# Scaled fp16 pairs in place of fp32r pairs in the projections of a gated two-branch attention kernel

## The chip, the cores and the metric

The kernel runs on one core of a Trainium2 chip. The time is device microseconds of one execution, on that core. A core has five engines that run their own instruction streams in order and meet at semaphores: TensorE (PE in the profile; its weight loads are listed apart as PEld), VectorE (DVE), ScalarE (ACT), GpSimdE (POOL) and SyncE (SP), which here only issues transfers. Matmuls write PSUM, which has eight banks of 512 fp32 columns; DVE and ACT read the results from there.

## The reference

Two attention branches read the same x (2048 tokens, 512 features) and are mixed by a gate. Both have 32 heads of 16 features.

```python
g = sigmoid((x * gate_w).sum(-1, keepdims=True))
a = A(x, wq, wk, wv, wo, beta)        # memory-augmented, four segments of 512 tokens
b = B(x, wqkv, wo_b)                  # plain softmax attention over all 2048 tokens
out = g * a + (1 - g) * b
```

In A, each segment has causal softmax attention inside the segment and a linear memory over the segments before it. With `phi(t) = t + 1 for t > 0, exp(t) otherwise`:

```python
q, k, v = x @ wq, x @ wk, x @ wv                 # split into heads and segments
a_dot = softmax(q @ k.T * 0.25 + causal) @ v
a_mem = (phi(q) @ M) / (phi(q) @ z + 1e-6)
o = sigmoid(beta) * a_mem + (1 - sigmoid(beta)) * a_dot
M, z = M + phi(k).T @ v, z + phi(k).sum()        # for the next segment
```

The weights of A's Q and K are larger than B's by a factor of 200, so the scores need about fp32 precision. All products with x are therefore made from pairs: each operand is split into a high and a low part, and three of the four products are summed (high-high, high-low, low-high).

## The kernel before, in words

x comes transposed, in four chunks of 512 tokens (`load_xt`), each as four slices of 128 features. The kernel has two stages.

The first stage, to about 375 us, makes the projections. `split_x` and `split` make the pairs: ACT copies the fp32 source into an fp32r tile (the high part), DVE subtracts that from the source (the low part). `v_job` projects 128 tokens onto all 512 columns of V with 12 matmuls (four feature slices times three products, `v_mm`, line 285) and ACT evicts the bank (line 293). `qk_job` projects one chunk of 512 tokens onto a group of 128 columns (8 heads) of Q or K with 12 matmuls (`qk_mm`, line 311). `qk_out` then turns the bank into an fp16 pair: ACT writes `st[:, 0] = b * sc` (line 323), DVE writes `st[:, 1] = b * sc - st[:, 0]` (line 326), where `sc` is a power of two per weight group, taken from the group's largest magnitude and x's. In A the same bank also gives phi: DVE takes the minimum with 0 (line 322), ACT the exponential of that, in place (line 325), and DVE adds the positive part (line 328). The pairs go to DRAM as images of Q and K, from which the attention reads.

The power of two comes from `x_abs` and `w_abs` (DVE: largest magnitude per partition), `w_top` (a matmul with the identity turns the column into a row, DVE takes the maximum) and `w_rng` (a matmul with ones spreads it over the partitions, DVE keeps the exponent bits and inverts). Only the outputs are scaled; the fp32r operands of the matmuls are not.

The order is written out by hand. First come the four slices of chunk 0 and of A's V weights: each is split as it lands, and its four matmuls, one for each of the first four V tiles, follow. Then come V tiles 0 to 15 of A; between them stand the splits of the next chunk, the gate's dot product (`dot_x`, DVE), the statistics, and POOL's weight loads. Then follow the eight Q and K jobs of B's first group, and 16 blocks (`blk`): each has one Q job and one K job of A, a read-out of the memory (`mem_out`, matmuls at line 397, which need phi of that block's Q job), its update (`mem_tr`, `mem_upd`, `mem_put`), and two or three jobs of B from the list `fill`. From block 4 on, `spill` strews score tasks of the first attention units among them (pairs of matmuls at line 535 with a DVE maximum at line 537). `misc` hands out PSUM banks, the least recently used first: eight in the V tiles, six in the first blocks, four from block 4 on.

The second stage is attention: for 32 steps, score matmuls (line 598), exponentials on ACT (line 604), products with V (line 620), and the maxima for the next step (lines 535 and 537). Nothing of it is touched by the change, but four last B jobs of `fill` stand in its first step.

Of the kernel before, what the change touches and what calls it, by code (L numbers as in the profile page):

```python
# [18 lines left out]
H = 32  # L19
# [10 lines left out]
TOP = 4.0  # L30
# [8 lines left out]
def gated_mix_kernel(ctx, tc, xt, wq, wk, wv, wo, beta, wqkv, wob, gate_w, out):  # L39
# [27 lines left out]
    XH = [xh[c // 2][:, c % 2] for c in range(NC4)]  # L67
# [3 lines left out]
    RAWV = [KBF[0][:, k] for k in range(4)] + flat + [RAW[:, n] for n in range(8)]  # L71
# [4 lines left out]
    XL = [X.tile([128, 4, C], FR, name=f"xl{c}") for c in range(NC4)]  # L76
    WV = [X.tile([128, 4, DM], FR, name=f"wv{s}") for s in range(2)]
    WS = [[[X.tile([128, 4, 128], FR, name=f"ws{w}{s}") for s in range(2)] for w in range(2)]]
# [7 lines left out]
    rng = P.tile([128, 2, 4, 2], FT, name="rng")  # L86
    xbd = P.tile([128, 1], FT, name="xbd")
# [35 lines left out]
    def raw_buf():  # L123
        i = cnt.get("raw", 0)
        cnt["raw"] = i + 1
        return RAWV[i if i < 6 else 6 + (i - 6) % 8]

# [13 lines left out]
    def constants():  # L141
# [10 lines left out]
        nc.vector.memset(ones, 1.0)  # L152
# [33 lines left out]
    def split_x(c, ks, eng=None):  # L186
        src = XS[c][:, ks]
        nc.scalar.activation(XH[c][:, ks], src, AF.Copy)
        nc.vector.tensor_tensor(XL[c][:, ks], src, XH[c][:, ks], op=OP.subtract)

# [67 lines left out]
    def load_wv(kd, k, eng=None):  # L258
        src, c0 = wcols(kd, 2)
        WR[k] = raw_buf()  # L260
        (eng or nc.gpsimd).dma_start(WR[k], src[k * 128:(k + 1) * 128, c0:c0 + DM])

    def split_wv(k):
        split(WV[0][:, k, :], WV[1][:, k, :], WR.pop(k))

# [9 lines left out]
    def split_w(n, kd, g, ws=(0, 1)):  # L275
        for w in ws:
            split(WS[n][w][0], WS[n][w][1], WR[kd, g][w])

# [9 lines left out]
    def v_out(b, kd, tt):  # L288
# [4 lines left out]
        nc.scalar.activation(vs[:, tl % 2, :, :E], b.rearrange("p (h e) -> p h e", h=H), AF.Copy)  # L293
# [21 lines left out]
    def qk_out(b, kd, g, w, c):  # L315

        sc = rng[:, "AB".index(kd), g, w:w + 1]
        st = X.tile([128, 2, C], HF, name="st", bufs=4)
        phi = kd == "A" and (c > 0 if w == 0 else c < NC4 - 1)
        if phi:  # L320
            ph = PHI[g, w, c] = X.tile([128, C], FT, name=f"phi{w}")
            nc.vector.tensor_scalar(ph, b, 0.0, None, op0=OP.min)
        nc.scalar.activation(st[:, 0], b, AF.Copy, scale=sc)  # L323
        if phi:
            nc.scalar.activation(ph, ph, AF.Exp)
        nc.vector.scalar_tensor_tensor(st[:, 1], b, sc, st[:, 0], op0=OP.mult, op1=OP.subtract)  # L326
        if phi:
            nc.vector.scalar_tensor_tensor(ph, b, 0.0, ph, op0=OP.max, op1=OP.add)
# [12 lines left out]

    def x_abs(c):
        if "x" not in ST:
            ST["x"] = X.tile([128, NC4], FT, name="xabs")
# [796 lines left out]
```

## Time and profile before

| | us |
|---|---|
| three runs | 1846.36, 1846.48, 1847.8 |
| median | 1846.48 |
| profiled execution | 1849.68 |
| its span, first to last instruction | 1848.0 |
| V tiles of A end, first B projection starts | 60.15 |
| PE busy | 1807.7 |
| DVE busy | 1591.2 |
| ACT busy | 1432.4 |
| POOL busy | 339.3 |

A row of the timeline gives the start, the time, the engine, the line of the kernel, the operation, what it writes and reads, and, in brackets, how long the engine stood idle before and what ended that wait. Several like instructions in a row are merged (x8); their time is from the first start to the last end. A matmul's row includes its way through the array, so the distance between starts is what a stream of them costs, not the row's time. A group of instructions has its total busy time and the mean of one in ns. The row of a tile or line has the shortest, median and longest time of one in ns. A row of the waits has the total, the number and the longest.

### The profile page before, as it was taken

How to read it: one execution, taken by the hardware profiler on the slowest of the kernel's cores; microseconds unless marked ns; L12 is line 12 of the kernel's file. 1: busy time of each engine (PE TensorE's matmuls, PEld its weight loads, DVE VectorE, ACT ScalarE, POOL GpSimd, SP SyncE). 2: the span in 40 equal slices, each digit the busy share in tenths (PEclk: the TensorE clock that was granted, in tenths of full speed). 3: DMA queues.
4: the chain of work that ended last, by engine and by line, in shares of the span. 5: the costliest groups of instructions: out<-in, count | busy, mean ns of one | idle time of the engine just before them, and what ended most of it. 6: DMA issues, size and time to landing. Idle time of an engine off the chain costs nothing.

```text
span 1848.0 us, 44286 instructions
## 1 busy us (share of the span) xinstructions
PE 1807.7 (98%) x17781; PEld 730.0 (40%) x17781; DVE 1591.2 (86%) x1772; ACT 1432.4 (78%) x2709; POOL 339.3 (18%) x691
## 2 busy tenths in 40 slices
PE   8999999899999999999999999999999999999998
PEld 6677777532222222333333333333333333333325
DVE  6334786699999999999999999999999999999942
ACT  4233333388989999989898989898989898989894
POOL 6100000101212010212121212121212121212122
PEclk9999999999999999999999999999999999999999
DMA  7554534332323222323232323232323232323111
GB/s 229 92 141 141 148 99 106 87 96 68 97 74 93 61 80 64 79 68 85 67 85 67 85 68 85 67 86 67 85 68 85 67 85 69 87 69 87 47 39 61
DMA packets 162482, 158.92 MB, mean 86 GB/s; under 512 B 40140, under 2 KB 126620, under 8 KB 162276
## 3 DMA queue, kind: packets, MB, share of 16 engines
q1 hardware_dynamic: 158692, 149.29, 29.1%
q0 software_dynamic: 3296, 6.27, 1.8%
q8 instruction: 140, 2.29, 0.5%
q14 instruction: 66, 0.54, 0.1%
q10 hardware_dynamic: 288, 0.52, 0.1%
HBM read 103.38 MB, written 50.86 MB: 83 GB/s over the span
## 4 chain that ended last, share of the span: by engine, by line
PE 80%; DVE 13%; ACT 4%; issue 2%; DMA 1%; SPq 0%; ACTq 0%; DVEq 0%; POOLq 0%
PE pvb L620 29%; PE tb L598 12%; DVE mxb L537 10%; PE sbk L535 10%; PE mb L598 6%; PE tb L311 3%; ACT raw L604 3%; PE pvb L311 2%; PE tb L705 2%; PE tb L285 2%; PE sbk L513 2%; PE sbk L285 2%; PE mb L705 1%; PE mb L311 1%; PE sbk L311 1%
## 5 line engine op out<-in xcount | busy, mean ns | idle before, releaser
L537 DVE TENSOR_REDUCE mxb<-sbk 128x2 f32<-128x1024 f32 x1024 | 1173.7, 1221 | 24.7 <-PE sbk L535 13.1
L604 ACT ACTIVATE raw<-tb 128x512 f32<-128x512 f32 x1557 | 884.5, 600 | 64.5 <-PE tb L598 30.9
L620 PE MATMUL pvb<-raw,vb 128*17 128x256 f32 (+1 forms) x8072 | 645.2, 388 | 0.0
L535 PE MATMUL sbk<-kb,qb 64*128 64x512 f16 x2048 | 552.8, 378 | 9.3 <-DVE mxb L537 8.3
L604 ACT ACTIVATE raw<-mb 128x512 f32<-128x512 f32 x780 | 468.2, 600 | 31.5 <-PE mb L598 14.4
L598 PE MATMUL tb<-qb,kb 64*128 64x512 f16 x1343 | 467.0, 381 | 1.2 <-ACT raw L604 0.8
L598 PEld LDWEIGHTS <-kb 64*128 64x128 f16 x2048 | 143.6, 93 | 414.4 <-issue 409.3
L620 PEld LDWEIGHTS pvb<-raw,vb 128*17 128x17 f32 x8072 | 138.0, 95 | 403.3 <-issue 393.8
L598 PE MATMUL mb<-qb,kb 64*128 64x512 f16 x678 | 258.2, 381 | 1.1 <-DVE st L326 1.0
L607 POOL TENSOR_SCALAR_AFFINE_SELECT raw<-raw 128x256 f32<-128x256 f32 (+1 forms) x320 | 115.3, 361 | 326.6 <-ACT raw L604 318.3
L535 PEld LDWEIGHTS <-qb 64*128 64x128 f16 x2048 | 137.3, 93 | 43.4 <-issue 33.5
L521 DVE TENSOR_REDUCE mx<-sbk 128x2 f32<-128x1024 f32 (+1 forms) x128 | 133.9, 1088 | 7.0 <-PE sbk L517 5.9
L620 PE MATMUL pvb<-raw,va 128*17 128x256 f32 (+2 forms) x1280 | 103.2, 383 | 3.8 <-ACT pvs L629 1.1
L664 POOL TENSOR_TENSOR o<-o,d 128x512 f32<-128x512 f32 x31 | 39.5, 1274 | 216.5 <-DMA d<-rd 175.9
L523 DVE TENSOR_REDUCE mx<-sbk 128x4 f32<-128x512 f32 x64 | 61.3, 958 | 12.4 <-PE sbk L517 12.4
L513 PE MATMUL sbk<-ka,qa 64*128 64x512 f16 (+3 forms) x512 | 70.5, 296 | 0.0
L598 PE MATMUL tb<-qa,ka 64*128 64x384 f16 (+3 forms) x340 | 61.7, 303 | 0.0
L652 POOL TENSOR_TENSOR rec<-rec,grow 128x16 f32<-128x16 f32 x24 | 5.3, 221 | 275.9 <-DVE rec L644 275.9
L323 ACT ACTIVATE st<-tb,rng 128x512 f16<-128x512 f32 x21 | 14.4, 687 | 53.0 <-PE tb L311 19.8
L517 PE MATMUL sbk<-cmask,crows 64*128 64x64 bf16 x1024 | 52.7, 189 | 0.0
L517 PEld LDWEIGHTS <-crows 64*128 64x128 bf16 x1024 | 46.4, 94 | 13.7
L445 POOL TENSOR_TENSOR mst<-mtmp,mst 128x136 f32<-128x136 f32 x8 | 3.6, 452 | 257.8 <-DVE mtmp L444 257.8
(330 smaller groups left out, 1732.1 us busy)
## 6 DMA issues: line engine op xcount, KB each, us to landing
vb<-vdB SPq DMA_DIRECT2D x16, 1088.0 KB
pd<-pvs SPq DMA_DIRECT2D x64, 256.0 KB
kb<-dB SPq DMA_DIRECT2D x60, 256.0 KB
dB<-st SPq DMA_DIRECT2D x64, 128.0 KB
dA<-st SPq DMA_DIRECT2D x64, 128.0 KB
o<-pd SPq DMA_DIRECT2D x64, 128.0 KB
d<-rd SPq DMA_DIRECT2D x63, 128.0 KB
kb<-dB SPq DMA_DIRECT2D x60, 128.0 KB
```

What stands on the lines that cost most here:

```text
L285: nc.tensor.matmul(b, (XH, XL)[xi][c][:, n % 4, tl * 128:(tl + 1) * 128], WV[wi][:, n % 4, :], start=n == 0, stop=n == 11)
L311: nc.tensor.matmul(b, WS[ws][w][wi][:, k, :], (XH, XL)[xi][c][:, k, :], start=n == 0, stop=n == 11)
L513: nc.tensor.matmul(b[:, j, c0:c0 + n], q_of(u)[r, p, i * 128:(i + 1) * 128], k_of(u, p)[r, :n], start=True, stop=False)
L517: nc.tensor.matmul(b[:, j, c0 + n - 128 + w.start:c0 + n - 128 + w.stop], crows[r, n2 - 1], cmask[r, n2 - 1, w], start=False, stop=n2 == 2)
L521: nc.vector.tensor_reduce(m[:, :, p, i], b[:, :, :n], axis=AX.X, op=OP.max)
L523: nc.vector.tensor_reduce(m[:, :, :, i], b.rearrange("q j (p k) -> q j p k", p=2)[:, :, :, :n], axis=AX.X, op=OP.max)
L535: nc.tensor.matmul(b[:, j], q_of(u)[r, p, i * 128:(i + 1) * 128], k_of(u, p)[r, kc * C:(kc + 1) * C], start=True, stop=True)
L537: nc.vector.tensor_reduce(MXB[u][:, :, p, i, kc], b, axis=AX.X, op=OP.max)
L598: nc.tensor.matmul(bs[j][:, c0:c0 + w], k_of(u, h // 2)[r, 128 * it:128 * it + 128], q_of(u)[r, h // 2, q0:], start=True, stop=True)
L604: nc.scalar.activation(pt, bs[j], AF.Exp, scale=AT["esc", kd, qd // 2])
L607: nc.gpsimd.affine_select(out=m, in_=m, pattern=[[1, 128]] if n < 2 else [[0, 2], [1, 128]], compare_op=OP.is_ge, fill=0.0, base=0, channe ...
L620: nc.tensor.matmul(PVB[32 * h:32 * h + E + 1, q0 + lo:q0 + hi], vt[:, it, 4 * q + h, :], pt[:, lo:hi], start=it == 0 and lo == 0, stop=it ...
```

## The change

The operands of the projections become fp16 pairs. fp16 has a narrow range, so each operand is first multiplied by an exact power of two that brings its largest magnitude to between 2^13 and 2^14 (`WIDE`). One scale is found for each chunk of x, for A's V weights, for B's V weights, and for each group of Q and K weights. The scales are found on the chip: `peak` on DVE, `top` and `spread` with the two small matmuls of before.

- `split` takes the scale from a tile row: ACT writes `hi = raw * up` in fp16, DVE writes `lo = raw * up - hi`.
- At the start, no slice is split before the peaks of all four slices of chunk 0 and of A's V weights are known. All eight high parts are then made, then all eight low parts, and the first four V tiles do their high-high products, then their high-low ones.
- For chunks 1 to 3, the peak is taken from the raw chunk some tiles ahead, then come `top`, `x_rng`, and the two halves of the split.
- Results are scaled back where they are evicted: V by `vr` on ACT, Q and K by `xr` and, for phi, by `back`.
- phi is made in another way: DVE writes the positive part `max(b * un, 0)`, ACT writes the exponential straight from the bank into a tile `phe`, and DVE adds `min(exp, 1)` to the positive part, from SBUF.
- `w_abs`, `w_top` and `w_rng` move earlier by some jobs, a step `w_esc` is new, and weight loads of A and B stand up to one block earlier. Twelve raw weight buffers come before the eight that share the space of x, where six did.
- High parts of x move from a lasting tile into the pool that is released before attention; fp16 halves their size.

```diff
-    def split(hi, lo, raw):
-        nc.scalar.activation(hi, raw, AF.Copy)
-        nc.vector.tensor_tensor(lo, raw, hi, op=OP.subtract)
+    def split(hi, lo, raw, up):
+        nc.scalar.activation(hi, raw, AF.Copy, scale=up)
+        nc.vector.scalar_tensor_tensor(lo, raw, up, hi, op0=OP.mult, op1=OP.subtract)
...
+    XH = [X.tile([128, 4, C], HF, name=f"xp{c}") for c in range(NC4)]
+    XL = [X.tile([128, 4, C], HF, name=f"xl{c}") for c in range(NC4)]
+    WV = [X.tile([128, 4, DM], HF, name=f"wv{s}") for s in range(2)]
+    WS = [[[X.tile([128, 4, 128], HF, name=f"ws{w}{s}") for s in range(2)] for w in range(2)]]
...
-            nc.vector.tensor_scalar(ph, b, 0.0, None, op0=OP.min)
+            ex = X.tile([128, C], FT, name="phe")
+            un = back[:, g, w, c:c + 1]
+            nc.vector.tensor_scalar(ph, b, un, 0.0, op0=OP.mult, op1=OP.max)
         nc.scalar.activation(st[:, 0], b, AF.Copy, scale=sc)
         if phi:
-            nc.scalar.activation(ph, ph, AF.Exp)
+            nc.scalar.activation(ex, b, AF.Exp, scale=un)
         nc.vector.scalar_tensor_tensor(st[:, 1], b, sc, st[:, 0], op0=OP.mult, op1=OP.subtract)
         if phi:
-            nc.vector.scalar_tensor_tensor(ph, b, 0.0, ph, op0=OP.max, op1=OP.add)
+            nc.vector.scalar_tensor_tensor(ph, ex, 1.0, ph, op0=OP.min, op1=OP.add)
...
+    def top(key):
+        s, n = ST[key]
+        b = misc()
+        nc.tensor.matmul(b[:n, :128], s[:, :n], ident, start=True, stop=True)
+        r = X.tile([4, 1], FT, name="wtop", bufs=2)
+        nc.vector.tensor_reduce(r[:n], b[:n, :128], axis=AX.X, op=OP.max)
+        d = X.tile([4, 4], FT, name="wdiag", bufs=2)
+        nc.vector.tensor_scalar(d[:n, :n], ident[:n, :n], r[:n], None, op0=OP.mult)
...
+    def spread(key, parts):
+        d, n = ST[key]
+        t = misc()[:, :n]
+        nc.tensor.matmul(t, ones[:n], d[:n, :n], start=True, stop=True)
+        c0 = 0
+        for e, u in parts:
+            w = e.shape[1]
+            nc.vector.tensor_scalar(e, t[:, c0:c0 + w], 2.0 ** -100, None, op0=OP.max)
+            nc.vector.tensor_scalar(e.bitcast(I32), e.bitcast(I32), 0x7F800000, None, op0=OP.bitwise_and)
+            nc.vector.reciprocal(u, e)
+            nc.vector.tensor_scalar(u, u, WIDE, None, op0=OP.mult)
+            c0 += w
...
     for k in range(4):
-        split_wv(k)
-        split_x(0, slice(k, k + 1))
+        peak(s8[:, 0, k:k + 1], WR["A", "v", k], AX.X)
+        peak(s8[:, 1, k:k + 1], XS[0][:, k], AX.X)
+    nc.vector.tensor_reduce(stat("first", 2)[:, :2], s8, axis=AX.X, op=OP.max)
+    top("first")
+    spread("first", [(ve[:, 0:1], vu[:, 0:1]), (xe[:, 0:1], xu[:, 0:1])])
+    for k in range(4):
+        for t, raw, up in ((WV[0], WR["A", "v", k], vu), (XH[0], XS[0][:, k], xu)):
+            nc.scalar.activation(t[:, k], raw, AF.Copy, scale=up[:, 0:1])
...
+    for n in range(8):
         for tt in range(4):
-            v_mm(vb[tt], tt, k)
+            v_mm(vb[tt], tt, n)
+    x_abs(1)
...
+        if c < 3:
+            if tl == 0:
+                top(("x", c + 1))
+            elif tl == 1:
+                x_rng(c + 1)
+                split_x(c + 1, slice(0, 2))
+            elif tl == 2:
+                split_x(c + 1, slice(2, 4))
+            elif c < 2:
+                x_abs(c + 2)
```

More of the change, by code (lines that the diff above doesn't have):

```diff
@@ L29 @@
 FAR = 2.0 ** 15
-TOP = 4.0
+TOP = 2.0
+WIDE = 2.0 ** 13
 EARLY = 6
```

171 lines of the change are left out of this document (101 added, 70 removed).

## The prediction

> **What bounds the kernel now.** I read the page first, then the busy times by stage, then the chain of waits of the stage that the change touches, and last the timeline at the three places where the change adds something.
>
> ```profile
> span 1848.0 us, 44286 instructions
> PE 1807.7 (98%) x17781; PEld 730.0 (40%) x17781; DVE 1591.2 (86%) x1772; ACT 1432.4 (78%) x2709; POOL 339.3 (18%) x691
> ```
>
> ```profile
> core 0: us, PE busy (x) PEld busy (x) DVE busy (x) ACT busy (x) POOL busy (x), PEclk, DMA share, GB/s
> 0.00:15.00 15.00, 7.71 (x18) 5.59 (x19) 7.59 (x21) 5.87 (x10) 5.00 (x19) 1.00 0.86 293
> 15.00:60.00 45.00, 42.04 (x179) 32.50 (x178) 30.84 (x39) 15.25 (x23) 30.85 (x55) 1.00 0.69 164
> 60.00:96.00 36.00, 31.26 (x144) 24.51 (x143) 13.04 (x26) 9.84 (x17) 2.15 (x3) 0.95 0.37 96
> 96.00:160.00 64.00, 63.54 (x310) 51.71 (x309) 25.75 (x56) 22.42 (x48) 3.90 (x6) 1.00 0.50 142
> 160.00:340.00 180.00, 175.50 (x914) 131.40 (x912) 130.88 (x220) 62.59 (x129) 8.01 (x14) 1.00 0.43 122
> 375.00:1848.00 1473.00, 1456.93 (x16057) 467.02 (x16056) 1363.53 (x1391) 1302.71 (x2460) 285.40 (x589) 1.00 0.28 75
> ```
>
> Everything the diff touches ends near 375 us; the 1473 us behind it are attention, with TensorE (PE) and VectorE (DVE) both over 90% busy, and run the same instructions afterwards. So the change is decided in the first 375 us. There PE is the full engine (63.54 of 64.00, 175.50 of 180.00), except at the start (7.71 of 15.00). From 160 to 340 DVE has 131 of 180 us, so it is second, with slack, but not much.
>
> ```profile
> by line: PE pvb L311 15.2%; PE tb L311 14.8%; PE tb L285 10.3%; PE mb L311 7.2%; issue 5.2%; DVE st L326 4.3%; PE sbk L311 3.8%; ACT st L323 3.6%; DVE mxb L537 3.5%; PE sbk L285 3.4%; PE sbk L535 2.8%; DVE phi L328 2.5%; PE tb L397 2.4%; PE
> 157.37 5.54 PE tb L285 x24
> ```
>
> This is the chain from 96 to 345 us (249 us). Projection matmuls (L285 for V, L311 for Q and K) hold 15.2+14.8+10.3+7.2+3.8+3.4 = 54.7% of it, 136 us. A run of 24 took 5.54 us: 0.231 us each, so about 590 of them lie on the chain.
>
> **Term 1: the matmul itself.** The code issues 1152 projection matmuls: 192 for A's V, 96 for B's first group, 816 in the 16 blocks, 48 in the first attention step. Their count stays; operands go from fp32r to fp16. No fp16 matmul over 128 rows is in this trace. The nearest rows are the scores, fp16 over 64 rows and 512 columns.
>
> ```profile
> L311 PEld LDWEIGHTS tb<-xh,ws x88: 186/188/334, 81.7 to 315.5; 128*128 128x128 f32 x88
> ```
>
> ```profile
> L535 PEld LDWEIGHTS <-qb 64*128 64x128 f16 x2048 | 137.3, 93 | 43.4 <-issue 33.5
> ```
>
> ```profile
> 424.92 0.39 PE L598 MATMUL tb<-qb,kb 64*128 64x512 f16 x1
> 424.98 0.55 PE L535 MATMUL sbk<-kb,qb 64*128 64x512 f16 x2
> 425.19 0.37 PE L598 MATMUL mb<-qb,kb 64*128 64x512 f16 x1
> ```
>
> The weight load falls from 188 to 93 ns. On the lower half of the rows the L535 matmul at 424.98 is followed by L598 at 425.19: 0.21 us from start to start, with new weights between. On the other half L598 at 424.92 is followed by the second L535, which ends at 424.98 + 0.55 = 425.53 and so starts near 425.15: 0.23 us. The bounds are thus 0.231 (no gain) and 0.21; I take 0.218, between the two fp16 rows, a gain of 13.5 ns. The 590 on the chain give -8.0 us, the 96 of B's first group -1.3 us.
>
> The Trainium skill (TensorE: Matmul & The Clock Gate, sections "Back-to-back issue gap" and "Weight-path perf modes") says that fast weight load is on for 128 weights of a type other than FP32, and gives 2.5 ns over the streaming time, 216 ns for 512 columns. By that figure the same 686 matmuls would give an estimated -10.5 us in place of -9.3; the trace's faster load agrees in direction, but no run here shows the 128-row period.
>
> **Term 2: the start.** Today each chunk of x and wv is split as it lands, and the first matmul needs one chunk of each.
>
> ```profile
> 10.78 0.62 ACT L188 ACTIVATE xh<-raw 128x512 fp32r<-128x512 f32 x1
> ```
>
> ```profile
> 6.63 1.22 PE L285 MATMUL tb<-wv,xh 128*128 128x512 f32 x2 [6.63 <-ACT xh L188]
> 14.22 0.63 PE L285 MATMUL pvb<-wv,xh 128*128 128x512 f32 x1
> 14.65 1.13 PE L285 MATMUL tb<-wv,xh 128*128 128x512 f32 x4
> 21.90 1.82 PEld L285 LDWEIGHTS sbk<-wv,xh 128*128 128x128 f32 x8
> 60.15 1.80 PEld L311 LDWEIGHTS mb<-xh,ws 128*128 128x128 f32 x8
> ```
>
> ```profile
> 50.51 0.28 DVE L365 TENSOR_REDUCE wtop<-sbk 3x1 f32<-3x128 f32 x1 [1.34 <-PE sbk L363]
> 50.83 0.22 DVE L367 TENSOR_SCALAR wdiag<-ident,wtop 3x3 f32<-3x3 f32 x1
> 50.96 1.26 DVE L353 TENSOR_REDUCE wabs<-raw 128x1 f32<-128x512 f32 x2
> 57.60 0.16 DVE L377 COPY xbd<-tb 128x1 f32<-128x1 f32 x1 [5.38 <-PE tb L375]
> 58.70 0.17 DVE L384 TENSOR_SCALAR rng<-wexp 128x2 f32<-128x2 f32 x1
> 19.46 2.28 DVE L345 TENSOR_REDUCE xabs<-xh 128x1 f32<-128x2048 f32 x1
> ```
>
> Afterwards no cast starts before the maximum over all four chunks is known. The last chunk is there at about 10.7 (its cast at 10.78 waited for no load). Eight peaks of 0.63 us (1.26 for two), paired with the landings, end near 12.1. The maximum over partitions (matmul, L365, L367) takes 0.4+0.3+0.3, then the spreading matmul 0.4, then eight small operations at 0.22 apiece (six from 57.60 to 58.87 take 1.27) 1.7: both scales stand at 15.4. The first x cast ends near 16.1, where the first matmul starts, against 6.63. The eight casts go out at 0.6 us each until 19.7; the first sixteen matmuls, which today run 0.43 apart in this phase (14.22 to 14.65), end near 22; sixteen hi-lo ones follow. DVE's eight low halves end at 22.5, and only then comes the peak of chunk 1 (2.28): 24.8. Its two matmuls and seven small operations lead to scales at about 28.5, and two ACT casts of 1.1 us with an eviction between them end at 31. V tile 4 needs them; it starts today at 21.90. That is 9 us, and it is ACT and DVE time that nothing covers.
>
> In tiles 4 to 15, PE runs 0.16 us per tile faster (12 x 13.5 ns), but it now waits in line at the statistics' matmuls: "top" of chunk 2 stands behind the peak of 2.28 (about 1.4 us of stall), the spreading behind the gate's dot product on DVE (0.9), B's first "top" behind DVE's low halves (2.2), chunk 3 little. That is 4.5 us, of which today's stalls (45.5 us from 14.65 to 60.15 for 176 matmuls worth 40.7) already hold a part. I put the end of A's V at 69, 8.8 later. The bounds: 3 if only the first start and its slower pace remain (192 x 0.218 from 16.1 is 58, the slow pace of the first matmuls adds 2 and stalls 3, which makes 63), 11 if all stalls add. What follows waits for this V in PE's order, so nothing gives it back.
>
> **Term 3: the exponential now reads PSUM.**
>
> ```profile
> 108.67 0.69 DVE L322 TENSOR_SCALAR phi<-pvb 128x512 f32<-128x512 f32 x1 [5.94 <-PE pvb L311]
> 109.44 0.69 ACT L323 ACTIVATE st<-pvb,rng 128x512 f16<-128x512 f32 x1 [2.91 <-DVE phi L322]
> 110.03 0.62 ACT L325 ACTIVATE phi<-phi 128x512 f32<-128x512 f32 x1
> 110.17 0.75 DVE L326 SCALAR_TENSOR_TENSOR st<-pvb,rng,st 128x512 f16<-128x512 f32 x1 [0.80 <-ACT st L323]
> 110.83 0.68 DVE L328 SCALAR_TENSOR_TENSOR phi<-pvb,phi 128x512 f32<-128x512 f32 x1
> ```
>
> ```profile
> 126.43 0.70 PE L397 MATMUL pvb<-mst,phi 128*128 128x136 f32 x4 [0.20 <-DVE phi L328]
> ```
>
> ACT's first read of the bank waits for DVE's read of it to end, though both only read (109.44 after 109.36): two engines take turns on a bank. Today the exponential works on phi in SBUF beside DVE's L326. Afterwards it reads the bank, so DVE's second half must wait for it: ACT's two reads end at 110.03 + 0.69 = 110.72 in place of 110.13, and L326, then the last phi step, come 0.58 later. The bank is free when it was (the last step no longer reads it), so PE's banks lose nothing. What is late next is the memory read-out L397, which in blocks 2 and 3 of each group comes straight after the second job's 12 matmuls: today 0.20 us of wait at 126.43. Afterwards phi comes 0.58 later and those 12 matmuls end 0.16 earlier: 0.9, so 0.75 more, in eight blocks; a pair of score matmuls (0.54) sometimes stands between and covers it. I take +4, with bounds 0 and +6.
>
> The Trainium skill (PSUM — Partial Sum Buffer, section "PSUM bank collisions raise a hardware error") says that the compiler adds a dependency between any two instructions on different engines that touch the same bank and partitions, reads included. The trace agrees: 0.08 us between the two reads.
>
> **Small terms.** The power-of-two work per weight group grows from five to six or eight DVE operations of 0.2: six groups, 3 us of DVE, mostly in slack (49 of 180 us idle): +0.5. Low halves go from 0.69 to 0.75 us and evictions of V from 0.60 to 0.69 (a scale from a register row, as L326 and L323 have): behind PE, 0. A weight load that follows a stall costs 0.093 in place of 0.188; ten to twenty such places: -1. The earlier weight loads move on POOL's queue, 18% busy: 0; without that cover a load of some us would stand ahead of its peak.
>
> **Sum.** 8.8 - 1.3 - 8.0 + 4 + 0.5 - 1 = +3.0 us. The profiled execution took 1849.68 with a span of 1848.0, the median of the runs is 1846.48; the sum is relative, so 1849.5 on the median. About 0.2% (3.7 us) is what a measurement of this kernel can tell from no change: the forecast is no change, on the slow side.
>
> **Rivals.**
> - *The matmul gain is worth its full count (faster).* For it: PE stands 63.54 of 64.00 busy. 912 x 13.5 ns = -12.3 with B's group, restarts -1, phi hidden to +2, start +7: -4.3, 1842. Against it: only 54.7% of the chain is projection.
> - *DVE takes over from 160 to 340 (slower).* Place: DVE's queue in these blocks. Its wait for ACT grows by 0.58 in each of some 17 phi jobs, 10 us, plus 3 of small operations, in 49 us of idle time, of which the row below holds 26 already. Where the rest is not usable, the 590 matmuls gain nothing in those blocks and a further 2 us go: 8.8 - 1.3 + 2.5 = +10, 1856.5. It decides once DVE is over nine tenths busy or waiting for ACT there.
> - *fp16 streams no faster than fp32r (slower).* The 0.23 row speaks for it. Terms 1 and the 2.4 in term 2 fall away: +15, 1861.
>
> ```profile
> DVE st L326 <- ACT st L323: 26.3, 27, 2.5
> ```
>
> **How the numbers follow.** Forecast 0.42, its own range 1846 to 1854; faster rival 0.32; DVE 0.16; no fp16 gain 0.10. The range 1840 to 1860 leaves out half of the faster rival's low tail and most of the last. Faster: 0.24 of the first rival and 0.02 of the forecast, 0.26. Slower: 0.18 of the forecast, 0.13 and 0.10 of the slower rivals, 0.41. Same: 0.33.
>
> **What would show it.** In the changed profile: first V matmul near 16, V tile 4 near 31, first B projection near 69; a run of 12 projection matmuls in 2.6 us, not 2.78; DVE's st step starting after the exponential's end, and L397's waits near 0.9; PE still full from 160 to 340. The prediction is wrong if the start costs under 5 us, if a run of 12 stays at 2.78, or if st starts before the exponential ends.

## The result, and the profile after

The changed kernel takes 1859.0 us (median of 4 runs, 1858.51 to 1863.63) against 1846.56 before: a ratio of 1.0072, 95% interval 1.006 to 1.0084. It is slower by 12.4 us, inside the predicted range of 1840 to 1860, but on the far side of the 1849.5 that was forecast. Executions of one kernel differ by how long PE's granted clock falls: the ten of the run with the exponential from SBUF, below, go from 1842.8 us at a mean clock of 0.999 to 1853.2 us at 0.995, so that a difference of 2 or 3 us between two medians can be the clock's.

The page of the changed kernel, in the two rows that answer to those of before:

```profile
span 1856.8 us, 44357 instructions
PE 1790.9 (96%) x17797; PEld 627.5 (34%) x17797; DVE 1607.6 (87%) x1842; ACT 1440.2 (78%) x2709; POOL 339.3 (18%) x691
```

PE is busy 17 us less than before (1807.7), and yet the span is 8.8 us longer: PE now waits. The spans differ by less than the medians because the profiled execution of before lay 3.1 us over its median, and the one after lies half a microsecond under its own.

In the changed kernel V's matmul stands in line 293 and its eviction in 302, the Q and K matmul in 320, the statistics' two matmuls in 371 and 382, the peak in 354, phi's steps in 333, 336 and 339, the two writes of `st` in 334 and 337, and the memory read-out in 429.

The busy times by stage, after (columns as before: PE, PEld, DVE, ACT, POOL, clock, DMA share, GB/s):

```profile
core 0: us, PE busy (x) PEld busy (x) DVE busy (x) ACT busy (x) POOL busy (x), PEclk, DMA share, GB/s
0.00:16.00 16.00, 1.17 (x4) 0.58 (x4) 9.84 (x32) 2.83 (x5) 2.89 (x10) 1.00 0.89 301
30.00:77.00 47.00, 37.49 (x156) 15.25 (x154) 34.08 (x60) 15.06 (x20) 30.44 (x54) 0.93 0.66 137
107.00:160.00 53.00, 50.09 (x261) 26.83 (x261) 24.77 (x57) 20.32 (x43) 3.89 (x6) 1.00 0.52 149
160.00:340.00 180.00, 168.88 (x926) 85.35 (x923) 126.15 (x222) 65.63 (x127) 6.74 (x11) 1.00 0.43 123
380.00:1856.00 1476.00, 1460.96 (x16091) 468.23 (x16089) 1366.02 (x1394) 1305.63 (x2464) 285.50 (x589) 1.00 0.28 75
```

The second stage is as it was (1461 of 1476 us busy). In the blocks PE was full and no longer is: 168.88 of 180, where it had 175.50. In the first 16 us it does next to nothing, and from 30 to 77 it is idle for 9.5 us.

The starts of three points in the first stage, read from the timeline of each profiled execution, and the span show where the time went. They are used for all runs below; "the blocks" means the stretch between the second column and the third, whose last jobs already stand in attention's first step.

| kernel | first B projection | A's first Q job | last projection job | span |
|---|---|---|---|---|
| before | 60.4 | 94.0 | 369.4 | 1848.0 |
| after | 77.4 | 107.5 | 379.5 | 1856.8 |
| fp16 pairs, no scales | 56.4 | 86.5 | 350.3 | 1826.5 |
| the same, exponential from PSUM | 55.7 | 87.5 | 354.3 | 1830.4 |
| the same, with a factor per partition | 55.5 | 87.3 | 359.5 | 1836.0 |
| after, exponential from SBUF | 71.9 | 105.4 | 368.2 | 1844.7 |
| after, third V buffer | 73.5 | 107.0 | 380.1 | 1855.9 |
| after, both | 71.1 | 102.9 | 364.8 | 1841.1 |
| after, constant scales for x and A's V | 61.1 | 94.5 | 366.4 | 1843.1 |
| the same, and both | 58.3 | 91.8 | 356.8 | 1833.8 |
| constants for chunk 0 and A's V only, and both | 63.7 | 93.5 | 358.7 | 1835.0 |
| after, beta's loads later | 72.9 | 106.3 | 378.1 | 1856.9 |
| A's V in fp32r, the rest in fp16 | 63.0 | 101.8 | 366.9 | 1843.2 |
| the same, DVE in another order | 63.9 | 105.2 | 370.0 | 1847.8 |

From before to after the start loses 13.5 us (94.0 to 107.5), the blocks gain 3.4 (275.4 to 272.0), and what follows gains 1.3, which may be part of the excess of before's profiled execution.

The timeline of PE in the first 80 us, after:

```profile
16.07 1.03 PE L293 MATMUL tb<-wv,xp 128*128 128x512 f16 x2 [2.22 <-ACT xp L822]
29.78 0.60 PE L293 MATMUL tb<-wv,xp 128*128 128x512 f16 x2 [0.18 <-ACT xp L255]
31.39 1.47 PE L293 MATMUL tb<-wv,xp 128*128 128x512 f16 x6 [1.01 <-ACT xp L255]
...
43.34 0.38 PE L371 MATMUL sbk<-ident,stat 128*2 128x128 f32 x2 [1.91 <-ACT xp L255]
43.65 2.91 PE L293 MATMUL sbk<-wv,xp 128*128 128x512 f16 x8
46.35 1.75 PE L293 MATMUL sbk<-wv,xl 128*128 128x512 f16 x4
...
67.53 2.87 PE L293 MATMUL sbk<-wv,xp 128*128 128x512 f16 x8 [3.34 <-ACT vb L302]
70.20 1.77 PE L293 MATMUL sbk<-wv,xl 128*128 128x512 f16 x4
...
77.39 1.90 PE L320 MATMUL pvb<-xp,ws 128*128 128x512 f16 x8
...
112.69 1.89 PE L293 MATMUL tb<-wv,xp 128*128 128x512 f16 x8
115.28 1.89 PE L293 MATMUL tb<-wv,xp 128*128 128x512 f16 x8
```

The first V matmul comes at 16.07 and tile 4 at 29.78, with its second half at 31.39. Then the V tiles fall behind: the first B projection starts at 77.39. Two of the tiles run at a slower rate (43.65 and 67.53: 2.9 us for eight matmuls that take 1.9 elsewhere). In the last two rows twelve matmuls take 2.59 us from start to start, 0.216 each.

One phi job in the blocks, after, on ACT, DVE and PE:

```profile
137.01 0.69 ACT L334 ACTIVATE st<-mb,xr 128x512 f16<-128x512 f32 x1 [4.05 <-DVE phi L333]
137.60 0.68 ACT L336 ACTIVATE phe<-mb,back 128x512 f32<-128x512 f32 x1
138.31 0.75 DVE L337 SCALAR_TENSOR_TENSOR st<-mb,xr,st 128x512 f16<-128x512 f32 x1 [1.33 <-ACT phe L336]
138.98 0.68 DVE L339 SCALAR_TENSOR_TENSOR phi<-phe,phi 128x512 f32<-128x512 f32 x1
139.81 1.17 PE L429 MATMUL sbk<-mst,phi 128*128 128x136 f32 x8 [1.10 <-DVE phi L339]
```

DVE's L337 starts at 138.31, when the exponential (137.60 + 0.68) has ended, and the memory read-out waits 1.10 us for phi. ACT's first write had ended at 137.70, so the exponential holds `st` up by 0.58 us; the same holds in all 24 phi jobs. The waits from 110 to 365 us (total, times, longest) show how often it happens:

```profile
DVE st L337 <- ACT phe L336: 32.3, 24, 1.4
PE mb L429 <- DVE phi L339: 2.9, 4, 1.0
PE pvb L429 <- DVE phi L339: 2.4, 2, 1.4
```

### The profile page after: what moved, and what is told of

It reads as the page before. It is cut to its first block, busy times and chain, and to the rows that moved or that the text cites. A ratio compares the mean times of both kernels' runs of the same rounds, so it can differ in the third digit from the quotient of the medians.

```text
span 1856.8 us, 44357 instructions
## 1 busy us (share of the span) xinstructions
PE 1790.9 (96%) x17797; PEld 627.5 (34%) x17797; DVE 1607.6 (87%) x1842; ACT 1440.2 (78%) x2709; POOL 339.3 (18%) x691
## 4 chain that ended last, share of the span: by engine, by line
PE 76%; DVE 15%; ACT 5%; issue 2%; DMA 1%; SPq 0%; POOL 0%; ACTq 0%; DVEq 0%; POOLq 0%
PE pvb L652 29%; PE tb L630 12%; DVE mxb L569 11%; PE sbk L567 10%; PE mb L630 6%; ACT raw L636 3%; PE tb L320 2%; PE tb L737 2%; PE sbk L545 2%; PE tb L293 2%; PE pvb L320 2%; PE mb L737 1%; PE sbk L293 1%; DVE st L337 1%; PE mb L320 1%
## 5 line engine op out<-in xcount | busy, mean ns | idle before, releaser
L636 ACT ACTIVATE raw<-tb 128x512 f32<-128x512 f32 x1557 | 884.7, 600 | 64.2 <-PE tb L630 30.8
L555 DVE TENSOR_REDUCE mx<-sbk 128x4 f32<-128x512 f32 x64 | 60.9, 951 | 12.4 <-PE sbk L549 12.4
L334 ACT ACTIVATE st<-tb,xr 128x512 f16<-128x512 f32 x30 | 20.6, 687 | 64.6 <-DVE phi L333 37.6
L320 PEld LDWEIGHTS <-ws 128*128 128x128 f16 x480 | 46.4, 98 | 59.8 <-issue 8.5
```

Source lines behind the costliest of these rows:

```text
L320: nc.tensor.matmul(b, WS[ws][w][wi][:, k, :], (XH, XL)[xi][c][:, k, :], start=n == 0, stop=n == 11)
L555: nc.vector.tensor_reduce(m[:, :, :, i], b.rearrange("q j (p k) -> q j p k", p=2)[:, :, :, :n], axis=AX.X, op=OP.max)
L636: nc.scalar.activation(pt, bs[j], AF.Exp, scale=AT["esc", kd, qd // 2])
```

## The experiments

The kernel before, run beside them on the same chips, took 1846.8 to 1847.3 us.

### What fp16 alone is worth

The kernel before with fp16 tiles for the pairs. It leaves out the scaling of the operands, so that small low parts lose bits.

```diff
-    XL = [X.tile([128, 4, C], FR, name=f"xl{c}") for c in range(NC4)]
-    WV = [X.tile([128, 4, DM], FR, name=f"wv{s}") for s in range(2)]
+    XH = [X.tile([128, 4, C], HF, name=f"xp{c}") for c in range(NC4)]
+    XL = [X.tile([128, 4, C], HF, name=f"xl{c}") for c in range(NC4)]
+    WV = [X.tile([128, 4, DM], HF, name=f"wv{s}") for s in range(2)]
...
```

> The kernel before with the projections' operands as fp16 pairs, without any scale (low parts lose bits, nothing else is left out). In the changed kernel a job of 12 matmuls starts 2.59 us after the last, before 2.78, so 16 ns less each. Theory (PE bounds the first stage, term 1): 590 to 912 matmuls gain 9 to 15 us, 1832 to 1838. Rival (DVE takes over in the blocks, so the gain stays within them): 1843 or more.

Measured 1828.3 us (1827.83 to 1828.97), ratio 0.9899 [0.9883, 0.9916]: 18.8 us faster, and more than the theory's 9 to 15. The weight load's group and the blocks of this run:

```profile
L311 PEld LDWEIGHTS <-ws 128*128 128x128 f16 x480 | 46.3, 98 | 56.9 <-issue 5.9
```

```profile
160.00:340.00 180.00, 170.24 (x918) 83.35 (x917) 134.41 (x224) 64.84 (x134) 11.94 (x20) 0.98 0.43 119
```

The load falls from 188 to 98 ns. The matmul's gain is 0.231 - 0.216 = 15 ns, and 1152 of them make 17.3 us: the gain counts on every projection and not only on those that the chain of waits passes through. By the table 11.6 us lie in the blocks (275.4 to 263.8; the 852 matmuls there at 15 ns are 12.8) and 7.5 ahead of them, where 288 matmuls give 4.3. Of the other 3.2 us 1.4 are a job that ran at a slow rate in before's profiled execution, at 81.8 us; the rest is not placed. So the changed kernel does not lack the gain; it loses 31 us elsewhere.

### The exponential, taken back to SBUF

```diff
-            nc.vector.tensor_scalar(ph, b, un, 0.0, op0=OP.mult, op1=OP.max)
+            nc.vector.tensor_scalar(ph, b, un, 1.0, op0=OP.mult, op1=OP.add)
...
-            nc.scalar.activation(ex, b, AF.Exp, scale=un)
+            nc.scalar.activation(ex, ph, AF.Exp, bias=neg1)
...
-            nc.vector.scalar_tensor_tensor(ph, ex, 1.0, ph, op0=OP.min, op1=OP.add)
+            nc.vector.scalar_tensor_tensor(ph, ex, 1.0, ph, op0=OP.min, op1=OP.max)
```

> The changed kernel with phi as max(t + 1, min(exp(t), 1)): DVE writes t + 1 to SBUF, ACT takes the exponential from there, so the bank is read as often as in the kernel before. Theory (term 3: the exponential's read of the bank holds up DVE and the read-out): 3 to 6 us less than the changed kernel, 1853 to 1856. Rival (the wait is hidden): within 1 us of it, 1858 to 1860.

Measured 1849.56 us (1842.79 to 1853.15, 10 runs), ratio 1.0009 [0.9994, 1.0024]: 9.4 us under the changed kernel, where the theory had 3 to 6. Other than the expectation says, the bank is read once less than in the kernel before: three times here, four times in both kernels, so that this form also frees it earlier. In the timeline DVE's write of `st` no longer waits for the exponential, only for ACT's first write:

```profile
135.09 0.75 DVE L339 SCALAR_TENSOR_TENSOR st<-mb,xr,st 128x512 f16<-128x512 f32 x1 [0.76 <-ACT st L336]
```

The blocks take 262.8 us in place of 272.0. The start of this execution is also 2 us shorter, so the 9.4 is not yet clean.

### A third buffer for V's stores

```diff
+    VS.append(X.tile([128, 2, H, E + 1], FT, name="vs2"))
...
-        vs = VS[(cnt["vs"] - 1) % 2]
+        vs = VS[(cnt["vs"] - 1) % 3]
```

> The changed kernel with a third buffer for evicted V tiles. In its profile the eviction of tile 12 starts at 66.80, 2.6 us after its last matmul, and PE stands 3.3 us and then runs slowly for one tile (1.7). Theory (the eviction waits for the transfer that stores tiles 8 and 9): 4 to 6 us less, 1853 to 1855. Rival (it waits for DVE's peaks, as the profile names it): 1858 to 1860.

Measured 1854.03 us (1851.08 to 1857.6), ratio 1.0035 [1.0022, 1.0048]: 5.0 less than the changed kernel. The wait before tile 13 shrinks from 3.34 to 0.82 us, and the tile runs at the usual rate:

```profile
65.37 1.89 PE L294 MATMUL sbk<-wv,xp 128*128 128x512 f16 x8 [0.82 <-ACT vb L303]
```

So V waited for a buffer whose store had not landed. In the changed kernel this row names another releaser for the late eviction of tile 12, whose matmuls had ended at 64.2:

```profile
66.80 0.69 ACT L302 ACTIVATE vb<-sbk,vr 128x512 f32<-128x512 f32 x1 [4.41 <-DVE stat L354]
```

The profile names the wait that came last by its records, a DVE peak that has nothing to do with this tile. The run shows that it was the store.

### What holds that store

The 12 loads of beta, moved in the program from V tile 13 to B's first projection. On POOL's queue that puts them behind the copies of the constant rows: the first is issued at 53.62 us in place of 49.63.

```diff
-        if tt == 13:
-            load_beta()
...
+        if n == 0:
+            load_beta()
```

> The changed kernel with the 12 loads of beta (0.5 KB each, in single elements) issued with B's first projection, behind the copies of the constant rows, and no longer at V tile 13. Theory: these loads hold the DMA engines at 55 to 60 us (busy share 0.89 for 3 GB/s) and with them the store of V tiles 8 and 9, whose buffer tile 12 waits for: the store lands by 61, tile 12 is copied out as its matmuls end, and the run ends 3 to 6 us below the changed kernel (1859.0). Rival: the copies of the constant rows into the K and Q tiles, which then come first, hold the store just as long: within 2 us of the changed kernel.

Measured 1855.7 us (1852.62 to 1858.62), ratio 1.0044 [1.0027, 1.0061]: 3.3 less, as the theory had it. Tile 12 is copied out at 64.02, right after its matmuls. From 55 to 60 us, first in the changed kernel and then in this run:

```profile
55.00:60.00 5.00, 4.17 (x21) 1.99 (x21) 2.17 (x7) 3.56 (x4) 2.02 (x3) 1.00 0.89 3
```

```profile
55.00:60.00 5.00, 4.17 (x20) 1.86 (x20) 2.42 (x7) 3.42 (x4) 5.00 (x8) 1.00 0.56 122
```

With beta's loads in flight the DMA engines are 89% busy and move 3 GB/s; with the copies ahead of them 56%, at 122 GB/s. The stretch of little traffic goes with the loads: in this run it comes from 60 to 65 us, 82% busy at 4 GB/s. Now the next store is late: ACT waits 3.42 us for it at 71.7, but PE does not. The first B projection starts at 72.9 in place of 77.4. But in the profiled executions of this run and of the one before, both near the top of their ranges, B's first group takes 33.4 and 33.5 us in place of 30.1 and gives most of it back. The timeline of this run says how: two jobs run at a slow rate, one after a wait of 1.98 us, one after the gate's column sums (32 matmuls of one column, 3.5 us).

```profile
77.99 3.43 PE L320 MATMUL sbk<-xp,ws 128*128 128x512 f16 x8 [1.98 <-DVE ve L386]
97.69 3.10 PE L320 MATMUL pvb<-xp,ws 128*128 128x512 f16 x8
```

In the changed kernel's profiled execution the same two places run at the full rate, after the same wait:

```profile
82.45 1.89 PE L320 MATMUL sbk<-xp,ws 128*128 128x512 f16 x8 [1.98 <-DVE ve L386]
100.61 1.89 PE L320 MATMUL pvb<-xp,ws 128*128 128x512 f16 x8
```

So one execution can lose 3.4 us there and another not, and for differences of this size the medians count: the store costs 3 to 5 us.

### Constant scales for x and A's V

The largest magnitudes of x and of A's V weights are not measured: their powers of two are constants, and the splits run as the data lands. Scales of the other weights stay measured.

```diff
-        peak(s8[:, 0, k:k + 1], WR["A", "v", k], AX.X)
-        peak(s8[:, 1, k:k + 1], XS[0][:, k], AX.X)
...
+    for e, u, v in ((ve[:, 0:1], vu[:, 0:1], 2.0 ** -4), (xe, xu, 2.0 ** -3)):
+        nc.vector.memset(e, v)
+        nc.vector.memset(u, WIDE / v)
+    for k in range(4):
+        split_wv("A", k)
+        split_x(0, slice(k, k + 1))
...
```

> The changed kernel without finding the scales of x and of A's V weights: they are constants (2^16 and 2^17), and the slices of chunk 0 and the weights are split as they land, as in the kernel before. Left out: the search for these five scales. Theory (term 2: the statistics of x ahead of the V tiles cost the start and all waits behind them, 16 us by the V stage's end): 15 to 18 us less than the changed kernel, 1841 to 1844, below the kernel before. Rival (the later stages wait for something else and take half of it back): 1849 to 1853.

Measured 1844.22 us (1838.33 to 1848.77), ratio 0.9982 [0.9972, 0.9992]: 14.8 less than the changed kernel, just short of the theory's 15 to 18, and 13.0 of them stand ahead of A's first Q job (107.5 to 94.5). The blocks stay at 271.9. The start is the largest single loss.

### Exponential and third buffer at once

The two edits above in one kernel.

```diff
+    VS.append(X.tile([128, 2, H, E + 1], FT, name="vs2"))
...
+            nc.scalar.activation(ex, ph, AF.Exp, bias=neg1)
```

> The changed kernel with the exponential read from SBUF and a third buffer for A's V stores at once. Theory: the exponential's cost lies in the blocks, so it shows here as 5 to 9 us against the run with the third buffer alone (1854.0): 1845 to 1849. Rival: what the exponential alone gave (9.4 us below the changed kernel) was the store stall of tile 12, absent in that profile by chance, and the two are one gain: then 1849 to 1851, no better than the exponential alone (1849.6).

Measured 1845.41 us (1841.97 to 1850.15, 10 runs), ratio 0.9995 [0.9984, 1.0005]. Against the third buffer alone that is 8.6 us less, so the two add, and by the medians the exponential's cost is 8.6 to 9.4.

### All three, and constants for the first chunk only

The first kernel has constant scales, exponential from SBUF and third buffer; the second takes constants only for x's first chunk and A's V weights, and measures chunks 1 to 3.

```diff
-    for e, u, v in ((ve[:, 0:1], vu[:, 0:1], 2.0 ** -4), (xe, xu, 2.0 ** -3)):
+    for e, u, v in ((ve[:, 0:1], vu[:, 0:1], 2.0 ** -4), (xe[:, 0:1], xu[:, 0:1], 2.0 ** -3)):
...
+            if tl == 0:
+                top(("x", c + 1))
...
```

> The changed kernel with constant scales for x and A's V, the exponential read from SBUF and a third buffer; the statistics and powers of two of the other weights, and the scales' use, stay. Theory: start and exponential are all the loss that matters, and they add: fixed start (1844.2) less 6 to 9 for the exponential gives 1835 to 1838, which leaves 7 to 10 us over fp16 pairs without scales (1828.3) for the weights' statistics, the small DVE work and the K/Q steps. Rival: the weights' statistics cost nothing on the path and the sum of the two is the whole loss: 1829 to 1832.

> As the run before in this call, but with constant scales only for x's first chunk and A's V; the largest elements of chunks 1 to 3 are measured on the chip as in the changed kernel. This splits the loss of the start. Theory: the first wait (first V matmul 16 and tile 4 at 30 us, against 22 before) is 7 to 9 us of it and the statistics between the tiles the rest, some 5 to 7 us: the end lies 5 to 7 us above the run with all constants. Rival: the stalls between the tiles hide once the start is early (the banks and stores have slack again): within 2 us of it.

Measured 1835.16 us (1831.39 to 1836.22), ratio 0.9929 [0.9912, 0.9945], and 1836.17 us (1834.33 to 1836.76), ratio 0.9936 [0.992, 0.9953]. The first is as the theory of the sum had it: 9.1 under the constant scales alone, and 6.9 over fp16 without scales. In the second the theory of the stalls falls: measuring chunks 1 to 3 costs 1.0 us, not 5 to 7. The stalls between the tiles have not gone, though. The first B projection comes 5.4 us later (63.7 against 58.3), but B's first group takes 29.8 us in place of 33.5. Two things make up this difference of 3.7. The first kernel waits in that group for the exponent of A's first weight group (a row of the first kernel):

```profile
63.41 3.15 PE L323 MATMUL sbk<-xp,ws 128*128 128x512 f16 x8 [1.99 <-DVE ve L389]
```

DVE's chain for it starts as V ends, and in the second kernel the later V hides it: 2.0 us. And the job behind that wait is slow, so that the first kernel has two slow jobs in the group and the second one: 1.7 us, which may be chance. Without that the stalls would cost 5.4 - 2.0 = 3.4 us, still under the theory. The wait ahead of the first matmul and of tile 4 is then the main cost of the start: 1845.4 - 1836.2 = 9.2 us.

### The exponential from PSUM, put into fp16 alone

The question turned round: fp16 without scales, with the changed kernel's form of phi.

```diff
-            nc.vector.tensor_scalar(ph, b, 0.0, None, op0=OP.min)
+            nc.vector.tensor_scalar(ph, b, 0.0, None, op0=OP.max)
...
-            nc.scalar.activation(ph, ph, AF.Exp)
+            nc.scalar.activation(ex, b, AF.Exp)
...
-            nc.vector.scalar_tensor_tensor(ph, b, 0.0, ph, op0=OP.max, op1=OP.add)
+            nc.vector.scalar_tensor_tensor(ph, ex, 1.0, ph, op0=OP.min, op1=OP.add)
```

> fp16 pairs without scales (1828.3), with one thing of the changed kernel put in: phi = min(exp(t), 1) + max(t, 0), whose exponential reads the PSUM bank behind ScalarE's copy into st, so that DVE's subtraction into st comes after both. It turns the question on the exponential round. Theory: it costs the blocks what taking it out gave in the changed kernel, 8 to 9 us: 1835 to 1838, and PE waits for phi's bank in the blocks as it does there. Rival: what the exponential's form cost came from the scales with it (another multiplication of t by a scale, the order of the small DVE work), not from the bank: 1828 to 1831.

Measured 1832.64 us (1831.9 to 1833.18), ratio 0.9925 [0.9908, 0.9942]: 4.3 over fp16 alone, between the two theories. The groups by shape, from 96 to 380 us, of this run and then of the changed kernel (busy time, mean ns of one):

```profile
L323 DVE TENSOR_SCALAR phi<-mb 128x512 f32<-128x512 f32 x8 | 5.5, 685 | 5.1 <-PE mb L311 5.1
L326 ACT ACTIVATE phe<-mb 128x512 f32<-128x512 f32 x8 | 4.7, 588 | 0.0
```

```profile
L333 DVE TENSOR_SCALAR phi<-mb,back 128x512 f32<-128x512 f32 x7 | 5.2, 748 | 5.7 <-PE mb L320 5.7
L336 ACT ACTIVATE phe<-mb,back 128x512 f32<-128x512 f32 x7 | 4.8, 679 | 0.0
```

The changed kernel's two operations take a factor from a column in SBUF (`back`, one value per partition). They are 63 and 91 ns longer.

### The factor per partition

The run before, with both factors read from a column of ones.

```diff
-            nc.vector.tensor_scalar(ph, b, 0.0, None, op0=OP.max)
+            nc.vector.tensor_scalar(ph, b, one, 0.0, op0=OP.mult, op1=OP.max)
...
-            nc.scalar.activation(ex, b, AF.Exp)
+            nc.scalar.activation(ex, b, AF.Exp, scale=one)
```

> The run with fp16 pairs without scales and the exponential from the PSUM bank (1832.6), with one thing more: both first steps of phi take their factor from a column of ones in SBUF, one value per partition, as the changed kernel takes its scale, and no longer a constant. In the changed kernel's rows the exponential with such a factor took 679 ns against 588 without, and phi's first step 745 against 685: 0.15 us for each of 24 phi jobs, 3.6 us if all of it shows. Theory: this is what makes the exponential dearer in the changed kernel (8 to 9 us) than here (4.3): 1834 to 1836.5. Rival: the rest comes from other small work of the scales in the blocks: 1832 to 1833.3.

Measured 1837.72 us (1836.66 to 1841.1), ratio 0.9953 [0.9939, 0.9966]: another 5.1 us, more than the theory's 3.6, and the rival is out. The rows of this run:

```profile
L323 DVE TENSOR_SCALAR phi<-mb,one 128x512 f32<-128x512 f32 x8 | 6.0, 746 | 5.1 <-PE mb L311 5.1
L326 ACT ACTIVATE phe<-mb,one 128x512 f32<-128x512 f32 x8 | 5.4, 680 | 0.0
```

The durations are those of the changed kernel, and so are the blocks: 272.2 us against 272.0. Both steps together cost fp16 alone 9.4 us, as much as taking the exponential back gave the changed kernel. The split into 4.3 for its place and 5.1 for its factor is less sure. The blocks of fp16 alone, of the run before and of this one (columns as above):

```profile
86.52:350.29 263.77, 252.13 (x1362) 123.98 (x1361) 172.59 (x295) 96.26 (x196) 15.82 (x26) 0.99 0.45 126
87.48:354.32 266.84, 249.90 (x1362) 123.40 (x1361) 172.40 (x295) 95.47 (x196) 15.82 (x26) 1.00 0.44 124
87.30:359.52 272.22, 253.33 (x1361) 124.11 (x1361) 173.85 (x295) 97.67 (x196) 15.84 (x26) 0.99 0.43 122
```

PE's idle time (length less busy time) is 11.6, 16.9 and 18.9 us: 5.3 more for the place, 2.0 more for the factor. Its busy time differs too, in the main because the first and the third execution have jobs at a slow rate there (2.3 us lost in one job and 2.9 in two) and the second has none. One of the two in the third follows a wait for phi:

```profile
260.03 1.17 PE L398 MATMUL tb<-mst,phi 128*128 128x136 f32 x8 [1.92 <-DVE phi L329]
262.10 3.08 PE L311 MATMUL mb<-xp,wv 128*128 128x512 f16 x8
```

The run before waits 1.77 us at this place and keeps the full rate. So of the 5.4 us by which the blocks grow from the second to the third 2.0 are waits and 2.9 the slow rate. Whether the factor's longer wait brings the slow rate on, or chance does, stays open.

Nor need a factor cost anything. With the exponential back in SBUF the changed kernel keeps the factor of DVE's first step (748 ns), and its exponential takes a bias per partition and is longer still. The group of that run, and the blocks of the changed kernel and of that run:

```profile
L338 ACT ACTIVATE phe<-phi,neg 128x512 f32<-128x512 f32 x24 | 17.1, 711 | 0.0
```

```profile
107.51:379.49 271.98, 251.59 (x1362) 124.29 (x1361) 175.62 (x307) 99.80 (x196) 15.88 (x26) 0.99 0.43 122
105.41:368.17 262.76, 250.58 (x1362) 124.11 (x1361) 176.12 (x307) 100.21 (x196) 15.89 (x26) 0.99 0.44 126
```

PE's idle time falls from 20.4 to 12.2 us, close to the 11.6 of fp16 alone (this form also frees the bank earlier). That fits a length that counts only while it stands between two readers of the bank; a run with the factor but without the exponential's new place was not made.

The Trainium skill (ScalarE: Activation LUTs, section "What ACT_TABLE_LOAD costs") says that each operand with one value per partition adds about 93 ns to an activation; the trace agrees: 588 to 680 ns.

### A's V in fp32r, the rest in fp16

A's V is split as it lands, without scales, as before; Q, K and B's V take scaled fp16 pairs, made meanwhile. The exponential reads SBUF. The second run has DVE's work in another order.

```diff
+        split32(WV32[0][:, k], WV32[1][:, k], WR["A", "v", k])
+        split_x32(0, slice(k, k + 1))
...
+        if tt == 12:
+            x_rng(0)
+            split_w(0, "B", 0)
...
+        if tt == 13:
+            split_x(0, slice(0, 2))
+            split_x(0, slice(2, 4))
```

> A's V stays in fp32r pairs, split as x and Wv land, as in the kernel before; Q, K and B's V take the scaled fp16 pairs, whose statistics are measured while A's V runs; the exponential reads SBUF. Theory: A's V ends near 61 to 66 us, the blocks gain as in the other fp16 runs: 1830 to 1838, below both kernels. Rival: the statistics and the second split of x are only moved, and DVE and ACT are late with B's first operands: the first B projection starts at 70 or later and the run ends at 1840 to 1848.

> As the run in which A's V stays in fp32r pairs (1844.0), with VectorE's work ahead of B's first projection in another order: x's largest elements are found by V tile 5, its fp16 pairs are made at tiles 10 to 14, and the gate's sums over x go behind them and into B's first group. There B's first group took 38.8 us against 30.2 in the run with fp16 pairs without scales, with waits for the second pairs of x. Theory: DVE's order was what cost these 8 us: 1834 to 1838. Rival: DVE has no room for two splits of x before B's projections in any order: 1841 or more.

Measured 1844.02 us (1842.28 to 1845.86), ratio 0.9981 [0.9971, 0.999], and 1848.3 us (1846.13 to 1851.73), ratio 1.0008 [0.9999, 1.0018]. The first is faster than both kernels, but by 0.2% only. Its time is the rival's, its place is not: V ends at 63.0, as the theory had it, and the loss lies behind it, in B's first group, which takes 38.8 us:

```profile
70.27 0.75 DVE L356 SCALAR_TENSOR_TENSOR st<-sbk,xr,st 128x512 f16<-128x512 f32 x1
```

```profile
71.07 3.36 PE L339 MATMUL sbk<-xp,ws 128*128 128x512 f16 x8 [5.29 <-DVE st L356]
```

The first Q job's `st` stands on DVE behind the second split of x (2.47 us from 67.88) and, ahead of that, the peaks of the weights, and the second job waits 5.29 us for it. The other order made this wait 5.87 us and the run slower, so its theory falls. An order that puts the whole of the second split behind the first jobs was not run.

## Why the prediction was right and wrong

Right was the sign: the start and the exponential outweigh the matmuls' gain, and none of the three signs of being wrong came. But the forecast was no change, and each term of its sum came out larger than it was put. That the time still fell inside the range is luck in part: the gain was 6.1 us larger and the losses 15.4, and the first hides some of the second:

| step | predicted | measured |
|---|---|---|
| fp16 matmuls, start and blocks, with restarts | -12.7 | -18.8 |
| scales of x and A's V at the start | +11.2 | +14.8 |
| exponential from PSUM, with its factor | +4 | +9.4 |
| weights' statistics, small DVE work, what else remains | +0.5 | +6.9 |
| sum | +3.0 | +12.3 |

The prediction's sum is regrouped here: its +8.8 for the start held 2.4 of the matmuls' gain. Measured are the differences of medians: fp16 alone to before; after to constant scales; the factor run to fp16 alone; constant scales with both edits to fp16 alone. They add to 12.3, against 11.9 between 1859.0 and 1847.1.

**Term 1, the matmul.** The step that failed is the count. The period was 0.216 us, between the 0.218 taken and the bound of 0.21. But "590 on the chain", 54.7% of it, was used as if the other projections gained nothing. PE was full in the blocks, so each of the projections there gained. (0.231 less 0.218 is also 13.0 ns, not 13.5, which is 0.3 us on the 686 matmuls.) The rival "full count" had this right, and its other terms wrong.

**Term 2, the start.** Its first half holds: 16.07 for 16, and for the 31 of tile 4, at which its second cast was to end, 31.39 (the tile's first two matmuls already start at 29.78). Its second half was mis-sized: A's V ended at 77.4, not 69. Tiles 4 to 15 took 47.3 us (29.78 to 77.08) for 144 matmuls worth 31.1. Of the 16.2 us between, 9.5 are idle PE, 3.4 two tiles at a slow rate, 1.9 the statistics' matmuls (six at 0.31), and most of the rest is the end of the last matmul ahead of each of the seven waits (a row of 0.38 us, where 0.22 lie between starts). The forecast had 6.9 for all of it (38.0 from 31 to 69, less 31.1). The three stalls that it named came: 1.19, 0.40 and 1.91 us ahead of the statistics' matmuls, 3.5 where it had 4.5. It followed DVE's queue and left out the waits for V's evictions (0.84, 0.82 and 3.34 us, the last for V's store, through ACT and a buffer), the slow rate after a wait, and the statistics' matmuls themselves.

**Term 3, the exponential.** The mechanism and the size of one job are as forecast: `st` starts at the exponential's end, 0.58 us late in each of the 24 jobs, phi is late, and the read-out waits about 1 us. The step that failed is the price of this delay: it was counted at the read-out alone, in eight blocks. From the run with the exponential in SBUF to the changed kernel the blocks grow by 9.2 us, and PE's idle time in them by 8.2. The read-out's waits for phi grow from 2.7 to 6.4, so this part, 3.7, is near the forecast's 4. The other 4.5 are waits that it took for nothing: for `st`, the last reader of the bank (2.4 more), for the memory's update (1.3 more), and others.

**Small terms.** "Mostly in slack" was wrong for B's first group: with constant scales and both edits PE waits 1.99 us there for DVE's chain of statistics. Where the 6.9 us lie is read, not tested: of the 7.3 between the two spans 5.3 stand ahead of A's first job (91.8 against 86.5), 2.0 in V and 3.3 in B's first group, where two jobs run slow and fp16 alone has none. How much of that is the statistics and how much the clock's chance stays open.

**The rivals.** "DVE takes over" has the nearest time, 1856.5, and most of the mechanism. DVE's waits for ACT from 160 to 340 us, after:

```profile
DVE st L337 <- ACT phe L336: 22.8, 17, 1.4
DVE st L337 <- ACT st L334: 15.2, 9, 9.4
```

With 2.6 us ahead of a weight split they are 40.6 us, 12.0 more than before (28.6); the rival had 10. DVE is then busy (126.2 us) or waiting for ACT in 93% of this stretch, 89% before, so its condition of nine tenths came. Of the matmuls' gain of 11.6 us the blocks keep 3.4; the rival had them keep nothing and lose a further 2. PE stays the fuller engine (168.9 of 180 us busy), and the start cost more than the rival's 8.8. "fp16 no faster" is out. And "PE still full from 160 to 340" is the forecast's own test that failed.

## What to carry to other kernels

A factor that is found from data at the head of a kernel costs the wait for the last of that data plus the chain that makes it, here 9 us; work at the head that needs no factor should come first, if its operands can be made without a second pass. Where PE is full, count a faster matmul on all matmuls of the stage, and price a step that is put between two readers of one PSUM bank at every wait that it lengthens, not only at the nearest. Pairs in fp16 without scales took 1828.3 us and beat both kernels; with scales found on the chip the best run was 1844.0.

## What the runs showed of the hardware

**PE can be slow after a wait.** The granted clock (third number from the end) in the changed kernel, in the two stretches around the slow tiles:

```profile
45.00:50.00 5.00, 4.16 (x14) 1.60 (x13) 4.89 (x5) 0.69 (x1) 4.64 (x9) 0.72 0.50 92
70.00:72.00 2.00, 2.00 (x6) 0.69 (x5) 1.67 (x3) 0.00 (x0) 0.00 (x0) 0.57 0.65 205
```

After waits of 1.91 and 3.34 us twelve matmuls took 4.45 us in place of 2.77, 1.7 us each time. A wait of 1.98 us was followed by the slow rate in one run and not in another, and so were the gate's one-column matmuls: a wait of 2 us cost 2 or 3.7. The Trainium skill (TensorE: Matmul & The Clock Gate, section "What's actually happening") says that the clock is halved after an idle window of about 3.4 us, and that this window runs free of the kernel; here the measurement differs, since 1.91 us of wait was enough. That the slow rate came and went between executions agrees with a window that runs free.

**Small loads can hold the DMA engines.** With twelve loads of 0.5 KB in flight they were 89% busy at 3 GB/s, and the buffer of a store of 544 KB issued at 55.83 was not free before 66.8.

**A factor per partition makes an operation longer.** It adds 91 ns to an activation and about 60 ns to DVE's operation on 512 columns. What that cost the kernel hung on the place of the operation: with the exponential in SBUF PE's idle time shows nothing of it.
